# Batch 1's steps, the weight differences, one gate difference and the batch loads at other places in an attention and feed-forward kernel

## The chip, the cores and the metric

One core of a Trainium2 chip runs the kernel. The metric is the time of one execution on the device, in microseconds (us); the median of three runs stands for a kernel. Beside it there is a profiled execution, whose trace gives the start and the length of every instruction. The engines are PE (matrix products), ACT (activation functions and copies), DVE (elementwise work and reductions), POOL (elementwise work, and the issue of DMAs that convert types) and SP (the issue of the other DMAs). Each engine works through its own instructions in the order of the program, and waits for others by semaphores.

## The reference

```python
def _attn_ref(q, k, v):                      # 8 batches, 8 heads, 576 tokens, 64 per head
    q_s = np.exp(q - np.max(q, axis=-1, keepdims=True))
    q_s = q_s / (np.sum(q_s, axis=-1, keepdims=True) + 1e-09)
    k_s = np.exp(k - np.max(k, axis=2, keepdims=True))
    k_s = k_s / (np.sum(k_s, axis=2, keepdims=True) + 1e-09)
    kv = np.einsum('bhsd,bhse->bhde', k_s, v)
    return np.einsum('bhsd,bhde->bhse', q_s, kv)

def _moe_ref(x, w_in, w_out, beta):          # x: (4608, 512), the heads side by side
    h = x @ w_in                             # w_in: (512, 2048)
    g = h * (1.0 / (1.0 + np.exp(-beta * h)))
    return g @ w_out                         # w_out: (2048, 512)
```

## The kernel before

The 576 tokens of a batch are 512 main tokens and a remainder of 64. The feed-forward part runs over nine slabs of 512 tokens: slab t (0 to 7) holds the main tokens of batch t, slab 8 the remainders of all eight. The attention of batch t + 1 is worked out while slab t runs, so that its result XT (the input of the slab, four pieces of 128 columns) is there when slab t + 1 starts.

**A slab.** Pass 1 (line 618) makes 16 tiles of the hidden layer, each by four matmuls of 512 columns; ACT applies the activation (GT), DVE multiplies by 1/beta (`scale_g`, L633) and adds up tiles into GS1 and GS2 (`g_sum1`, `g_sum2`). Pass 2 of slab 0 is a plain output product of 64 matmuls (`pass2_group`). In the other slabs pass 2 (`pass2_fast`, line 695) is a Strassen-like scheme of seven products of 16 matmuls (256 columns, L703). It uses sums of quarters of WOUT (WSUM, made by `w_sum`, L685), differences of quarters (`w_diff`, L691, in place in WOUT) and differences of halves of GT (`g_diff`, L673, in place in GT). The first three products use GS1 and GS2, the fourth and fifth untouched quarters of GT. The sixth needs `g_diff(0)`, the seventh `g_diff(1)`. DVE collects three products in TS (L754, L757, L761).

**The attention of a batch.** The main tokens of q, k and v are loaded to QF, KF and VF (`load_main`), the remainders to QRF, KRF and VRF. ACT takes exponentials (EQ, EK, EKR, EQR). `norm_main` normalises the queries of two head pairs: a reduce (L331) and a reciprocal (L332) on DVE, a multiply (L333) on POOL or DVE. The normalised queries are transposed to QT by PE for batches 1 and 2 (`t_steps`, with a copy on ACT), by a DMA from SP for later ones (`turn`, L482); the query remainders go to QTR (`turn_rem`, L489). `cast_v` casts v to VB, `cast_vr` its remainder. `kv_steps` are the key-value products; behind each pair DVE takes a reciprocal (RC, L437) and scales (KVD, L417). `out_step` multiplies KVD by QT, and DVE or ACT evacuates the result to XT (L455). `outr_steps` does the same for the remainders of two batches, with QTR, into XT8.

**What sets the order.** The whole program is one list, written in the order of emission; each engine gets its part of it. Attention steps have due places in ticks, in the list `todo`: a matmul of pass 1 and one of slab 0's output product count one tick, one of `pass2_fast` 32/56 (so a product is 9.14 ticks, and pass 2 is ticks 64 to 128). After each matmul `tick` emits the steps that are due. `spread(steps, lo, hi)` gives steps even places from lo to hi. `on(n, f)` hangs other work at place n of pass 2: `at(0)` is its start, `at(1)` stands behind the second product and the copy of the first, `at(3)` behind the third product, `at(4)` to `at(7)` behind the following ones. Loads are issued in program order by SP, which waits at each until the buffer is free. The lines that the change touches are the due places (506 to 519 and 795 to 811), the gate differences in `pass2_fast` (763), the weight differences and casts of v (820 to 837), the end of slab 0 (844 to 862), and the hooks (884 to 918).

## Time and profile before

| | |
|---|---|
| median of 3 runs | 293.38 us (293.07 to 293.47) |
| the profiled execution | 295.68 us |
| its span in the trace | 293.9 us |
| TensorE clock granted, mean of the span | 0.983 |
| HBM read / written | 36.71 MB / 9.44 MB |
| slowest DMA of a batch load, issue to landing (VF, 1 MB) | 10.9 us (median of 6) |

The span runs from the first to the last instruction of the trace; the time of the execution holds what lies around it too. Rows of the timeline read: start and length in us, engine, line, operation, out<-in, shape, count, and in brackets how long the engine was idle ahead of it and which instruction ended that. PEld is the loading of weights into PE, which runs beside PE. Rows of the list of waits read: total us, how many times, the longest. SPq and POOLq are the issuing of DMAs. A buffer's number is left out of its name.

### The profile page before, as it was taken

The page shows a single profiled execution, that of the slowest core. Times are in us where ns is not written, and L with a number is a line of the kernel's source. Part 1 is how long each engine was busy: PE and PEld are TensorE (multiplying, and loading weights), DVE is VectorE, ACT ScalarE, POOL GpSimd, SP SyncE. Part 2 cuts the span into 40 slices and gives each one's busy share as a digit, 9 for nine tenths or more (in the row PEclk, how much of TensorE's full clock was granted, in tenths as well). Part 3 has the DMA queues.
Part 4 walks back from the last instruction along what each step waited for, and adds up shares of the span by engine and source line. Part 5 has one row for each costly group of instructions (what it writes and reads, how often), then busy time and mean ns, then how long its engine had stood idle before and what let it go on. Part 6 is the DMA issues. An engine that isn't in the chain of part 4 may idle for free.

```text
span 293.9 us, 4673 instructions
## 1 busy us (share of the span) xinstructions
PE 272.2 (93%) x1819; PEld 168.9 (57%) x1845; DVE 198.9 (68%) x408; ACT 186.1 (63%) x284; POOL 70.6 (24%) x84
## 2 busy tenths in 40 slices
PE   7899968998799979999894999999999999999994
PEld 2444424457654766458551587568656854784583
DVE  5953594499746896987844678697768747654851
ACT  4787574898468954789562695688567457218610
POOL 2870070353600094600830007200600100000000
PEclk9999999999999998999997899999999999999999
DMA  7999999997960069955999004701430040003005
GB/s 219 307 206 206 269 340 349 227 354 256 333 194 0 0 92 347 244 180 186 273 349 249 0 8 94 171 0 39 88 144 2 0 163 0 2 0 143 2 1 142
DMA packets 57205, 45.39 MB, mean 154 GB/s; under 512 B 26448, under 2 KB 56160, under 8 KB 56160
## 3 DMA queue, kind: packets, MB, share of 16 engines
q1 hardware_dynamic: 52352, 40.38, 48.3%
q0 software_dynamic: 4224, 4.19, 8.6%
q10 hardware_dynamic: 608, 0.53, 0.5%
q8 instruction: 14, 0.23, 0.3%
q14 instruction: 7, 0.06, 0.1%
HBM read 36.71 MB, written 9.44 MB: 157 GB/s over the span
## 4 chain that ended last, share of the span: by engine, by line
PE 62%; DVE 16%; DMA 10%; POOL 3%; ACT 3%; SPq 3%; issue 2%; POOLq 0%
PE PS L375 36%; PE PS L703 25%; DMA QF<-in_q_dram 5%; DMA WOUT<-in_moe_w_out_dram 4%; DVE QS L331 4%; DVE GT L673 4%; SPq L482 2%; DVE KVD L417 1%; DVE GT L633 1%; ACT GT L627 1%; POOL VB L348 1%; DMA QTR<-EQR 1%; DVE GS L666 1%; POOL WIN L548 1%; ACT EQ L300 1%
## 5 line engine op out<-in xcount | busy, mean ns | idle before, releaser
L375 PE MATMUL PS<-XT,WIN 128*128 128x512 bf16 x559 | 130.8, 384 | 1.8 <-DVE XT L455 0.8
L627 ACT ACTIVATE GT<-PS,BETA 128x512 bf16<-128x512 f32 x144 | 98.9, 688 | 46.8 <-PE PS L375 46.8
L375 PEld LDWEIGHTS PS<-XT,WIN 128*128 128x128 bf16 x576 | 53.5, 98 | 62.6 <-DVE XT L455 2.3
L633 DVE TENSOR_SCALAR GT<-GT,RB 128x512 bf16<-128x512 bf16 x144 | 54.2, 390 | 45.3 <-ACT GT L627 44.8
L333 POOL TENSOR_TENSOR EQ<-EQ,QI 128x1024 bf16<-128x1024 bf16 (+1 forms) x17 | 28.9, 1702 | 123.9 <-DVE QI L332 106.7
L703 PE MATMUL PS<-WOUT,GT 128*128 128x256 bf16 x256 | 35.1, 273 | 4.5 <-DVE RC L437 3.7
L703 PE MATMUL PS<-WSUM,GT 128*128 128x256 bf16 x256 | 32.2, 280 | 0.0
L703 PE MATMUL PS<-WOUT,GS 128*128 128x256 bf16 x256 | 30.3, 273 | 0.2
L703 PEld LDWEIGHTS PS<-WSUM,GT 128*128 128x128 bf16 x256 | 25.7, 101 | 4.7 <-issue 0.3
L703 PEld LDWEIGHTS PS<-WOUT,GS 128*128 128x128 bf16 x256 | 24.9, 98 | 3.6
L703 PEld LDWEIGHTS PS<-WOUT,GT 128*128 128x128 bf16 x256 | 24.8, 98 | 3.6 <-DVE TS L757 0.2
L733 ACT COPY O2S<-PS 128x512 f32<-128x512 f32 x16 | 9.3, 584 | 25.0 <-PE PS L703 23.5
L331 DVE TENSOR_REDUCE QS<-EQ 128x16 f32<-128x1024 bf16 (+1 forms) x20 | 19.9, 994 | 4.4 <-ACT EQ L300 4.4
L673 DVE TENSOR_TENSOR GT<-GT 128x2048 bf16<-128x2048 bf16 x16 | 22.6, 1453 | 0.0
L375 PE MATMUL PS<-VB,EK 128*128 128x129 bf16 x128 | 21.3, 220 | 1.2 <-DVE VB L348 1.1
L666 DVE TENSOR_TENSOR GS<-GT 128x512 bf16<-128x512 bf16 (+2 forms) x32 | 22.3, 697 | 0.0
L300 ACT ACTIVATE EQ<-QF 128x512 bf16<-128x512 f32 x32 | 17.9, 619 | 6.3 <-DMA QF<-in_q_dram 6.3
L455 ACT CAST XT<-PS 128x512 bf16<-128x512 f32 x18 | 10.4, 582 | 16.8 <-PE PS L375 16.7
L741 DVE TENSOR_TENSOR O2S<-TS,PS 128x512 f32<-128x512 f32 x16 | 10.7, 679 | 13.4 <-PE PS L703 13.4
L348 POOL CAST VB<-VF 128x512 bf16<-128x512 f32 x24 | 18.1, 752 | 1.9
L300 ACT ACTIVATE EK<-KF 128x512 bf16<-128x512 f32 x32 | 18.0, 617 | 0.3 <-DMA KF<-in_k_dram 0.3
L703 PE MATMUL PS<-WSUM,GS 128*128 128x256 bf16 x128 | 16.6, 274 | 1.0 <-DVE GS L661 0.8
(77 smaller groups left out, 240.5 us busy)
## 6 DMA issues: line engine op xcount, KB each, us to landing
out_dram<-O2S SPq DMA_DIRECT2D x8, 1024.0 KB, 4.1
QF<-in_q_dram SPq DMA_DIRECT2D x6, 1024.0 KB, 7.0
KF<-in_k_dram SPq DMA_DIRECT2D x6, 1024.0 KB, 8.6
VF<-in_v_dram SPq DMA_DIRECT2D x6, 1024.0 KB, 10.9
KF<-in_k_dram SPq DMA_DIRECT2D x8, 256.0 KB, 5.6
VF<-in_v_dram SPq DMA_DIRECT2D x8, 256.0 KB, 5.6
WIN<-in_moe_w_in_dram POOLq DMA_DIRECT2D x4, 512.0 KB, 7.4
WOUT<-in_moe_w_out_dram POOLq DMA_DIRECT2D x4, 512.0 KB, 15.6
```

Source lines behind the costliest of these rows:

```text
L300: add(ACTE, lambda e, o=o, a=a: e.activation(o, a, ACT.Exp), r=[(name + "f", i, hp)], w=[("e" + name, i, hp)])
L331: add(DVE, lambda e: e.tensor_reduce(s_, a, AX.X, ALU.add), r=ks, w=[("qs", i, hp0)])
L333: add(eng, lambda e: e.tensor_tensor(a, a, vb, ALU.mult), r=ks + [("qi", i, hp0)], w=ks)
L348: add(eng, lambda e: (e.copy if eng == ACTE else e.tensor_copy)(o, a), r=[("vf", i, hp), ("vone", i)], w=[("vb", i, hp)])
L375: add(PE, lambda e: e.matmul(o, l, r_, start=start, stop=stop), r=r, w=w, bank=[bk])
L455: add(eng, lambda e: (e.copy if eng == ACTE else e.tensor_copy)(XT[i][:, hp, :], PS[bk][:, :]), r=[("ps", bk)], w=[("xt", i, hp)], bank=[bk])
L627: add(ACTE, lambda e: e.activation(GT[:, f, :], PS[bk][:, :], ACT.Silu, scale=BETA[:, f:f + 1]), r=[("ps", bk), "beta"], w=[("gt", f, 0), ...
L633: add(DVE, lambda e: e.tensor_scalar(GT[:, f, :], GT[:, f, :], RB[:, f:f + 1], None, ALU.mult), r=k + ["rb"], w=k)
L666: add(DVE, lambda e: e.tensor_tensor(GS2[:, i:i + n, :], GT[:, i:i + n, :], GT[:, i + NG:i + NG + n, :], ALU.add), r=[k_ for f in (i, i + ...
L673: add(DVE, lambda e: e.tensor_tensor(gv(f, th, NG), gv(f, th, NG), gv(f, 1 - th, NG), ALU.subtract), r=gk(f, 0, NG) + gk(f, 1, NG), w=gk(f ...
L703: add(PE, lambda e, l=l, r_=r_, st=st, u=u, i=i: e.matmul(PS[bk][:, 256 * u:256 * u + 256], l, r_, start=st, stop=end and i == NG - 1, ski ...
L741: add(DVE, lambda e: e.tensor_tensor(o, ts, bank3(bk), ALU.add), r=["ts", ("ps", bk)], w=w, bank=[bk])
```

## The change

In slab 0, batch 1's steps go from ticks 89 to 127 to ticks 104 to 126 of the output product, with the last two key-value and output steps behind it; its query load waits for the third piece of WOUT, not the first; two weight sums go ahead of its norms. In slab 1 both weight differences go ahead of pass 1. In slabs 1 and 2 `norm_main` goes one hook later, `g_diff(0)` stands behind the norms and `g_diff(1)` behind the key-value scalings, by a due place of its own; batch 2's steps and the last steps of batches 3 and 4 move by some ticks. Batch 3's casts of v wait until slab 2 has scaled its first tile. In slab 3 the exponentials of batch 5's keys, its casts, the load of batch 6 and the query remainders go later, behind batch 5's norms and transposes; the load of batch 7 goes to slab 4. The remainder products of batches 2 and 3 (`outr_steps(3)`) go from ticks 40 to 56 to ticks 72 to 88 of slab 4.

```diff
-        def cast_v(b, hp, eng=POOL):
+        def cast_v(b, hp, eng=POOL, after=()):
...
-                r=[("vf", i, hp), ("vone", i)], w=[("vb", i, hp)])
+                r=[("vf", i, hp), ("vone", i)], w=[("vb", i, hp)], after=after)
...
             if b == 2:
-                s = spread(t_steps(b, (0, 1), MB, ACTE), 96, 99) + spread(k01, 99, 102)
-                s += spread(k23, 102, 106) + spread(t_steps(b, (2, 3), MB, ACTE), 108, 111)
-                return s + spread(x[0:2], 107, 108) + spread(x[2:4], 116, 120)
+                s = spread(t_steps(b, (0, 1), MB, ACTE), 104, 107) + spread(k01, 107, 110)
+                s += spread(k23, 110, 113) + [(113.5, lambda: g_diff(1))] + spread(x[0:2], 114, 116)
+                s += spread(t_steps(b, (2, 3), MB, ACTE), 116.5, 119)
+                return s + spread(x[2:4], 122, 125)
             if b == 3:
-                return (spread(k01, 97, 101) + spread(k23, 101, 105) + spread(x[0:2], 109, 112)
-                        + spread(x[2:4], 119, 122))
-            return spread(k01, 92, 98) + spread(k23, 98, 104) + spread(x, 108, 122)
+                s = spread(k01, 97, 101) + spread(k23, 101, 105) + [(105, lambda: g_diff(1))]
+                return s + spread(x[0:2], 110, 113) + spread(x[2:4], 120, 123)
+            return spread(k01, 93, 97) + spread(k23, 97, 101) + spread(x, 105, 122)
...
-            g_diff(0)
-            g_diff(1)
+            if t not in (1, 2):
+                g_diff(0)
+                g_diff(1)
...
-                        for hp, x in enumerate((89, 95, 100, 105))]
-                todo += [(101, one(exp_kr_s, 1))]
...
+                        for hp, x in enumerate((105, 110, 114, 117))]
+                todo += [(104, one(exp_kr_s, 1))]
...
-                    todo += spread(outr_steps(2 * t - 5), 40, 56) if t < 6 else spread(
-                        outr_steps(7), 60, 76)
+                    todo += spread(outr_steps(2 * t - 5), *((72, 88), (40, 56), (60, 76))[t - 4])
...
-            elif t == 2:
-                for hp in range(NHP):
-                    cast_v(3, hp)
+                w_diff(0)
+                w_diff(1)
...
-                    if t == 1 and n in (5, 10):
-                        w_diff(n // 10)
+                    if t == 2 and n == 2:
+                        for hp in range(NHP):
+                            cast_v(3, hp, after=P.writer[("gt", 0, 0)])
...
-                load_main("qf", qt_h, QF, 1, split=4, after=P.writer[("wout", 3, 0)])
+                load_main("qf", qt_h, QF, 1, split=4, after=P.writer[("wout", 11, 0)])
...
+                w_sum(0)
+                w_sum(2)
                 for hp in range(NHP):
                     norm_main(1, hp, 1, POOL if hp else DVE)
-                w_sum(0)
-                w_sum(2)
...
             if t == 1:
...
-                on(1, norm_main, 2, 0, 2, POOL)
-                on(2, norm_main, 2, 2, 2, POOL)
+                on(2, norm_main, 2, 0, 2, POOL)
+                on(3, norm_main, 2, 2, 2, POOL)
+                on(3, g_diff, 0)
             elif t == 2:
                 on(0, exps, 3)
-                on(1, norm_turn, 3, 0)
-                on(2, norm_turn, 3, 2)
+                on(2, norm_turn, 3, 0)
+                on(3, norm_turn, 3, 2)
+                on(3, g_diff, 0)
...
+            elif t == 3:
+                on(0, exp_k, 4)
+                on(0, exp_kr, 4)
+                on(0, exp_q, 5)
+                on(3, norm_turn, 5, 0)
+                on(4, norm_turn, 5, 2)
+                on(5, exp_k, 5)
+                on(5, exp_qr)
+                on(5, casts, 5)
+                on(5, load, 6)
+                on(7, norm_turn_rem)
+                on(7, load_rem, "qrf", qt_h, QRF, 4)
...
-                if b + 2 < B:
-                    on(0, load, b + 2)
+                if t == 4:
+                    on(0, load, 7)
```

Three places show how the instructions move. The first is DVE's order in slab 0, from the last scaled tiles to the first cast of v (before).

```order
L633 TENSOR_SCALAR GT<-GT,RB 128x512 x2
L331 TENSOR_REDUCE QS<-EQ 128x8
L332 RECIPROCAL QI<-QS 128x8
L333 TENSOR_TENSOR EQ<-EQ,QI 128x512
L331 TENSOR_REDUCE QS<-EQ 128x8
L332 RECIPROCAL QI<-QS 128x8
L331 TENSOR_REDUCE QS<-EQ 128x8
L332 RECIPROCAL QI<-QS 128x8
L331 TENSOR_REDUCE QS<-EQ 128x8
L332 RECIPROCAL QI<-QS 128x8
L685 TENSOR_TENSOR WSUM<-WOUT 128x2048 x2
```

The same place of DVE in the changed kernel:

```order
L634 TENSOR_SCALAR GT<-GT,RB 128x512 x2
L686 TENSOR_TENSOR WSUM<-WOUT 128x2048 x2
L331 TENSOR_REDUCE QS<-EQ 128x8
L332 RECIPROCAL QI<-QS 128x8
L333 TENSOR_TENSOR EQ<-EQ,QI 128x512
L331 TENSOR_REDUCE QS<-EQ 128x8
```

The two weight sums, which read all of WOUT, moved from behind the norms of batch 1's queries to ahead of them.

The second is DVE's order in pass 2 of slab 2, from the copy of the first product (before).

```order
L754 COPY TS<-PS 128x512
L331 TENSOR_REDUCE QS<-EQ 128x16
L332 RECIPROCAL QI<-QS 128x16
L757 TENSOR_TENSOR TS<-TS,PS 128x512
L331 TENSOR_REDUCE QS<-EQ 128x16
L332 RECIPROCAL QI<-QS 128x16
L761 TENSOR_TENSOR TS<-TS,PS 128x512
L673 TENSOR_TENSOR GT<-GT 128x8x256 x2
L437 RECIPROCAL RC<-PS 128x2
L417 SCALAR_TENSOR_TENSOR KVD<-PS,RC,MASK 128x128 x2
```

In the changed kernel DVE has there:

```order
L755 COPY TS<-PS 128x512
L758 TENSOR_TENSOR TS<-TS,PS 128x512
L331 TENSOR_REDUCE QS<-EQ 128x16
L332 RECIPROCAL QI<-QS 128x16
L762 TENSOR_TENSOR TS<-TS,PS 128x512
L331 TENSOR_REDUCE QS<-EQ 128x16
L332 RECIPROCAL QI<-QS 128x16
L674 TENSOR_TENSOR GT<-GT 128x8x256
L437 RECIPROCAL RC<-PS 128x2
L417 SCALAR_TENSOR_TENSOR KVD<-PS,RC,MASK 128x128 x2
```

One gate difference stands ahead of the key-value scalings, where there were two; the other follows the second pair of scalings. Each norm's reduce and reciprocal moved behind one more subtraction.

The third is SP's order from the store of slab 2's output (`out_dram`) to that of slab 3's (before).

```order
L643 DMA out_dram<-O2S 128x2048
L268 DMA QF<-in_q_dram 128x8x256
L268 DMA KF<-in_k_dram 128x8x256
L268 DMA VF<-in_v_dram 128x8x256
L275 DMA KRF<-in_k_dram 64x8x64 x2
L275 DMA VRF<-in_v_dram 64x8x64 x2
L275 DMA QRF<-in_q_dram 64x8x64 x2
L268 DMA QF<-in_q_dram 128x8x256
L268 DMA KF<-in_k_dram 128x8x256
L268 DMA VF<-in_v_dram 128x8x256
L482 DMA_TRANSPOSE QT<-EQ 128x8x128 x2
L489 DMA_TRANSPOSE QTR<-EQR 128x4x128
```

In the changed kernel SP has there:

```order
L644 DMA out_dram<-O2S 128x2048
L482 DMA_TRANSPOSE QT<-EQ 128x8x128 x2
L268 DMA QF<-in_q_dram 128x8x256
L268 DMA KF<-in_k_dram 128x8x256
L268 DMA VF<-in_v_dram 128x8x256
L275 DMA KRF<-in_k_dram 64x8x64 x2
L275 DMA VRF<-in_v_dram 64x8x64 x2
L489 DMA_TRANSPOSE QTR<-EQR 128x4x128
L275 DMA QRF<-in_q_dram 64x8x64 x2
L644 DMA out_dram<-O2S 128x2048
```

The transposes of batch 5's queries moved ahead of the load of batch 6; the remainder's transpose stays behind it; the load of batch 7 follows the store.

More of the change, by code (lines that the diff above doesn't have):

```diff
@@ L795, in bass_efficient_attn_shen__then__act_swish_beta_kernel @@
                 todo = [(x, steps(t_steps, 1, (hp,), NOW, ACTE))
-                        for hp, x in enumerate((89, 95, 100, 105))]
-                todo += [(101, one(exp_kr_s, 1))]
-                todo += [(x, one(exp_k, 1, hp, 1)) for hp, x in enumerate((102, 106, 111, 116))]
-                todo += [(x, one(cast_v, 1, hp, DVE)) for hp, x in enumerate((104, 107, 112, 118))]
+                        for hp, x in enumerate((105, 110, 114, 117))]
+                todo += [(104, one(exp_kr_s, 1))]
+                todo += [(x, one(exp_k, 1, hp, 1)) for hp, x in enumerate((111, 115, 118, 122))]
+                todo += [(x, one(cast_v, 1, hp, DVE)) for hp, x in enumerate((112, 117.5, 120, 125))]
                 todo += [(x, steps(kv_steps, 1, (hp,), NOW))
-                         for hp, x in enumerate((109, 115, 121, 127))]
-                todo += [(x, steps(out_step, 1, hp, NOW, ACTE)) for hp, x in enumerate((119, 125))]
+                         for hp, x in enumerate((116, 119, 124))]
+                todo += [(x, steps(out_step, 1, hp, NOW, ACTE)) for hp, x in enumerate((121, 126))]
             elif t < 4:
@@ L858, in bass_efficient_attn_shen__then__act_swish_beta_kernel @@
                     todo.pop()[1]()
+                go(kv_steps(1, (3,), NOW))
                 go(out_step(1, 2, NOW, ACTE))
```

10 lines of the change are left out of this document (1 added, 9 removed).

## The prediction

> **What bounds the kernel now.** I read the page first, then the list of waits of PE, then the timeline at every place where PE stood still.
>
> ```profile
> PE 272.2 (93%) x1819; PEld 168.9 (57%) x1845; DVE 198.9 (68%) x408; ACT 186.1 (63%) x284; POOL 70.6 (24%) x84
> PE PS L703 <- DVE RC L437: 3.7, 2, 2.2
> PE PS L375 <- DMA QTR<-EQR: 3.7, 1, 3.7
> PE PS L373 <- POOL EQ L333: 1.6, 2, 1.1
> PE PS L375 <- DVE VB L348: 1.1, 2, 0.7
> ```
>
> PE works for 93% of the span, so PE bounds the kernel, and what can be gained is its waits and the time it runs at a lower clock. The next rows are the first product of pass 2 in slabs 1 to 4, and, from the chain of work, in slab 5.
>
> ```profile
> 65.11 2.00 PE L703 MATMUL PS<-WSUM,GS 128*128 128x256 bf16 x14
> 97.32 2.05 PE L703 MATMUL PS<-WSUM,GS 128*128 128x256 bf16 x16
> 129.73 2.05 PE L703 MATMUL PS<-WSUM,GS 128*128 128x256 bf16 x16
> 167.04 2.05 PE L703 MATMUL PS<-WSUM,GS 128*128 128x256 bf16 x16
> 195.61 4.07 PE PS L703 x36
> ```
>
> From one to the next it is 32.2, 32.4, 37.3 and 28.6 us. The last one has no wait worth a line, so about 28.6 us is what a slab needs, and the first three lose 3.6, 3.8 and 8.7. The clock is part of it (columns: stretch, length, busy time and count of PE, PEld, DVE, ACT, POOL, granted clock, DMA share, GB/s):
>
> ```profile
> 111.00:112.00 1.00, 1.00 (x7) 0.69 (x6) 0.00 (x0) 0.54 (x1) 0.94 (x2) 0.50 1.04 359
> 163.00:164.00 1.00, 1.00 (x5) 0.36 (x3) 0.39 (x2) 0.54 (x1) 0.00 (x0) 0.50 0.00 0
> ```
>
> Behind the two longest waits (2.2 and 3.7 us) PE runs at half clock; stretch by stretch it is from 109.7 to 113.1 and from 159.0 to 164.3, so 1.7 and 2.6 us are lost on top of the waits.
>
> **Slab 0.** Batch 1's steps now stand behind 41 matmuls of the output product. What comes with it: batch 1's queries load behind the third piece of WOUT, not the first, and DVE adds the two weight sums, which need the last piece, ahead of the four query norms.
>
> ```profile
> L554 POOL DMA_DIRECT2D WOUT<-in_moe_w_out_dram x4: 770/781/795, 14.4 to 16.6; - x4
> DMA to landing us min/median/max: 12.5/15.6/20.3
> 30.16 5.56 PE L375 MATMUL PS<-WOUT,GT 128*128 128x512 bf16 x24
> 29.62 1.22 DVE L685 TENSOR_TENSOR WSUM<-WOUT 128x2048 bf16<-128x2048 bf16 x1
> 39.41 3.54 DVE L685 TENSOR_TENSOR WSUM<-WOUT 128x2048 bf16<-128x2048 bf16 x2
> 33.95 0.69 DVE L331 TENSOR_REDUCE QS<-EQ 128x8 f32<-128x512 bf16 x1 [2.52 <-ACT EQ L300]
> 35.66 0.23 PEld L373 LDWEIGHTS PS<-IDB,EQ 128*128 128x128 bf16 x4 [0.44 <-DVE EQ L333]
> ```
>
> PE's waits in front of batch 1's transposes (1.6 on POOL, 0.44 on DVE) and of its first key-value product (0.7) go, 2.7 us in all. The pieces of WOUT land from 26.9 (14.4 + 12.5) to 36.9 (16.6 + 20.3), 3.3 apart, with 1 MB of queries moving among them. Without those I take 2.7 apart (if the shares went by bytes, 1.5 MB of WOUT to 1 MB of queries, it would be 2.0): third at 32.3, last at 35.6 once the queries run beside it. DVE then ends the sums at 35.6 + 2 x 1.22 = 38.1 and the first norm (1.7 from its reduce at 33.95 to the transpose that waited for it, at 35.66) at 39.8. PE, at 0.217 a matmul, reaches the transpose at 30.2 + 41 x 0.217 = 39.1: it waits 0.7. The second norm ends on POOL 0.6 after PE wants it, and the remainder cast VRS, behind three multiplies on POOL, is 0.7 late. So 2.0 is added for 2.7 removed. With the last piece at 36.9 as now it is 3.3, and with the sums at 3.54 us 4.4. **Term: 0**, between a gain of 2.7 and a loss of 3.4 (the last with a half-clock stretch).
>
> **Slab 1.** The weight differences leave the busy end of pass 1 for its start.
>
> ```profile
> 56.88 1.21 DVE L691 TENSOR_TENSOR WOUT<-WOUT 128x2048 bf16<-128x2048 bf16 x1
> 53.08 0.35 DVE L633 TENSOR_SCALAR GT<-GT,RB 128x512 bf16<-128x512 bf16 x1 [1.85 <-ACT GT L627]
> 67.91 0.39 PE L703 MATMUL PS<-WSUM,GS 128*128 128x256 bf16 x2 [0.80 <-DVE GS L661]
> 77.92 0.27 PE L703 MATMUL PS<-WOUT,GT 128*128 128x256 bf16 x1 [1.49 <-DVE RC L437]
> L673 DVE TENSOR_TENSOR GT<-GT x4: 1624/2157/2691, 72.9 to 107.2; 128x2048 bf16<-128x2048 bf16 x4
> 135.92 2.35 DVE L673 TENSOR_TENSOR GT<-GT 128x2048 bf16<-128x2048 bf16 x2
> ```
>
> Two of 1.21 us go into a gap of 1.85; the 0.6 over is made up in the 0.5 us that DVE is idle at each following tile, so the wait of 0.80 goes. In pass 2 both gate differences stand ahead of the key-value scalings that PE waits for: 4.3 us together while POOL multiplies and casts, 2.35 where POOL is idle (135.92). After the change one stands ahead, and PE's wait of 1.49 goes with 0.4 of shorter ones behind it. The second difference, now uncontended since batch 3's casts moved to slab 2, ends about when its product wants it, and delays the next evacuation, for which PE waits some 0.5. **Term: -2.2**, between -1.2 and -2.6.
>
> **Slab 2.** Same move, with transposes by DMA.
>
> ```profile
> 104.28 3.48 SPq L482 DMA_TRANSPOSE QT<-EQ  x2
> QT<-EQ SPq DMA_TRANSPOSE x1, 4.5
> 102.35 3.88 POOL L333 TENSOR_TENSOR EQ<-EQ,QI 128x1024 bf16<-128x1024 bf16 x2 [23.43 <-DVE QI L332]
> 133.57 0.69 DVE L757 TENSOR_TENSOR TS<-TS,PS 128x512 f32<-128x512 f32 x1 [1.05 <-PE PS L703]
> 102.67 1.21 DVE L331 TENSOR_REDUCE QS<-EQ 128x16 f32<-128x1024 bf16 x1
> 116.33 3.57 PEld L375 LDWEIGHTS PS<-XT,WIN 128*128 128x128 bf16 x18 [0.63 <-DVE XT L455]
> ```
>
> Now the norm stands behind the first subtraction, which starts 3.84 after the pass (133.57 - 129.73), at 101.2. DVE in a row: subtraction 0.7, reduce 1.2, reciprocal 0.25, and the same again, to 105.4; one gate difference 2.1, to 107.5; the scalings 1.5, to 109.0; the second difference 1.2 to 2.1; then evacuation 0.6, 0.7, reduce 1.2, reciprocal 0.25, evacuation 0.6: the last input tile of slab 3 is there at 113.6 to 114.5, now 116.3. PE meanwhile wants the transposed queries at 107.3: their multiply ends 1 us later than now, at 105.2, and the transpose takes 3.3 to 4.5 us, so PE waits till 108.6 to 109.8, then has 4.3 us of work, which ends at 112.9 to 114.1, so DVE's chain is later. **Term: -1.8**; -2.7 if the second difference is fast, -0.3 if the clock halves again.
>
> The Trainium skill, page "SBUF — State Buffer", section "Who interferes with whom", says that a VectorE instruction with two SBUF inputs and a GpSimd one that reads SBUF exclude each other for a whole instruction, and this speaks against the change, since the remaining difference starts together with POOL's multiply. By that rule the difference would end 1.0 us later whenever POOL's 1.94 us came first, and the sum would be 1 us worse; the four differences of the row above took 1.6 to 2.7 us, and I stay with their middle.
>
> **Slabs 3 and 4.** In slab 3 batch 4's output step comes three ticks (0.6 us) earlier, but what it waits for does not.
>
> ```profile
> 140.46 0.38 PE L703 MATMUL PS<-WOUT,GT 128*128 128x256 bf16 x2 [0.78 <-DVE KVD L417]
> 147.73 8.70 SPq L482 DMA_TRANSPOSE QT<-EQ  x2
> QT<-EQ SPq DMA_TRANSPOSE x1, 9.7
> 156.47 1.27 SPq L489 DMA_TRANSPOSE QTR<-EQR  x1
> 159.01 0.23 PE L375 MATMUL PS<-QTR,KVD 128*128 128x64 bf16 x1 [3.67 <-DMA QTR<-EQR]
> 145.41 1.89 PE L375 MATMUL PS<-XT,WIN 128*128 128x512 bf16 x8
> 180.48 7.88 PE PS L375 x49
> 77.37 2.90 SPq L275 DMA_DIRECT2D VRF<-in_v_dram  x2
> 69.52 0.37 SPq L268 DMA_DIRECT2D QF<-in_q_dram  x1
> ```
>
> PE's wait there grows as much as the later wait of 0.44 shrinks, and the four key exponentials and the remainder's (2.8 us on ACT) now stand ahead of the last evacuation: **+0.4**, at most +1.5. Slab 4 is the large one. Pass 1 takes 167.04 - 145.41 = 21.6 us there and 195.61 - 180.48 = 15.1 in slab 5, with the same work: the 6.5 between them are the wait of 3.67 for the transposed remainder and the half clock behind it. The remainder's products now stand at tick 72, in pass 2, and the transposes of batch 5 no longer queue behind two batch loads on SP. PE will be at tick 72 at 145.8 + 15.0 + 1.5 = 162.3. On SP the remainder's transpose now follows one whole load, issued from about 145.2; the same loads in slab 1 took from 69.5 to 80.3 to issue, so it goes out at 156.0 and lands 2.5 us later, as at 156.47, or up to 9.7 later, as the transpose issued at 147.73 behind three loads. I take 160.5, in time. Batch 6's casts on POOL now fall beside the end of pass 1, for which I allow 0.3. **Term: -6.2**, or next to nothing if it lands at the slow end.
>
> **Sum.** 0 - 2.2 - 1.8 + 0.4 - 6.2 = -9.8: the span goes from 293.9 to 284.1. The profiled execution took 295.68 us, the median of the runs shown is 293.38; the difference of 2.3 I leave as it is, so the forecast is 293.4 - 9.8 = **283.6 us**. Slabs 5 to 8 stay as they are.
>
> **Rivals.** (1) *The weight sums hold up batch 1.* With WOUT's last piece at 36.9 and the sums at 3.54, PE waits 36.9 + 3.5 + 1.7 - 39.1 = 3.0 at the first transpose and 1.4 behind it, and a half-clock stretch costs 1.7: slab 0 loses 3.4, 287.0 us. For it: the sums wait for the last piece by construction; against it: the queries no longer share the DMA with the third piece. (2) *Slab 2 keeps its half clock*, since the transposes replace the scalings as the wait: 1.5 worse, 285.1. For it speaks that the 4.5 us landing alone makes 2.4 us of wait; against it that the wait of 1.49 in slab 1 left the clock at 1.00. (3) *The remainder's transpose lands at the slow end*, 165.7: a wait of 3.4 and 2.6 of half clock give 6.0 back, 289.6. (4) *Slower than before by that same wait*: all is lost when the remainder lands 7.2 us (9.8 less 2.6) past tick 72, at 169.5, which needs the transpose stuck on SP till 160 behind loads whose ring is full; at 171 the time is 294.9. (5) *The waits only change names* and each engine's total stands: 293.4.
>
> The Trainium skill, page "TensorE: Matmul & The Clock Gate", section "Part 1: The HAM clock gate (the "warmup" mystery)", has the half clock come after at least one idle window of about 3.4 us. Here 2.2 us of waiting were enough (clock 0.50 at 111), so by that rule the stretch in slab 2 had another cause and would stay: 1.5 us more, the same as rival 2.
>
> **How the numbers follow.** Forecast 0.60 (281.5 to 285.5: the terms of slabs 0, 1 and 2, each uncertain by about 1 and independent, make 2 either way), rival 1 0.13, rival 2 0.10, rival 3 0.12, rival 4 0.03, rival 5 0.02. The range of 280.5 to 288.5 holds the forecast and rivals 1 and 2; downward it goes half the way to the best bounds of slabs 0, 1, 2 and 4 together (-2.7 - 2.6 - 2.7 - 6.5 = -14.5, without the 0.4, 278.9). About 0.2% is what a measurement of this kernel can tell from no change. Faster is everything but rivals 4 and 5: 0.95; same 0.02; slower 0.03.
>
> **What would show it.** Right: in the waits of PE no line for QTR, the lines for RC gone or under 0.5 us, clock 1.00 everywhere from slab 1 on, and 30.0, 30.6 and 31.5 us between the first products of slabs 1 to 4. Wrong: PE waiting for norms in slab 0 by more than 2.5 us, a clock of 0.50 in any slab, or QTR still named.

## The result, and the profile after

The changed kernel took **284.73 us** (median of 4, 284.34 to 285.11), the kernel before, run beside it, 293.43 (293.07 to 294.58): a ratio of 0.9697, 95% interval 0.9667 to 0.9727. The profiled execution took 284.34 us with a span of 282.5, so the two profiled executions differ by 11.34 us and the two medians by 8.7. That gap is taken up in the experiments.

First comes PE's row on the page of the changed kernel, and then rows of its list of waits (total us, times, longest):

```profile
PE 270.2 (96%) x1845; PEld 168.6 (60%) x1845; DVE 195.1 (69%) x408; ACT 186.1 (66%) x284; POOL 67.6 (24%) x84
```

```profile
PE PS L375 <- DVE KVD L417: 2.3, 4, 1.2
...
PE PS L375 <- DMA QT<-EQ: 1.2, 2, 0.9
PE PS L704 <- DVE GS L662: 1.1, 2, 0.7
PE PS L375 <- DVE VB L348: 0.9, 2, 0.5
```

No row of the list names QTR, RC or POOL's EQ any more. From pass 2 of slab 1 on, what is left is 0.7 us for the sums of GT in slab 1, 0.9 and 0.3 for the transposed queries in slab 2, and 1.2 for the scalings in slab 3, beside two waits of 0.2 and 0.35. The timeline of PE has the first products of pass 2 in slabs 1 to 5:

```profile
63.71 1.69 PE L704 MATMUL PS<-WSUM,GS 128*128 128x256 bf16 x14
...
94.39 2.05 PE L704 MATMUL PS<-WSUM,GS 128*128 128x256 bf16 x16
...
124.11 2.05 PE L704 MATMUL PS<-WSUM,GS 128*128 128x256 bf16 x16
...
155.06 1.69 PE L704 MATMUL PS<-WSUM,GS 128*128 128x256 bf16 x14
...
184.09 2.05 PE L704 MATMUL PS<-WSUM,GS 128*128 128x256 bf16 x16
```

In the kernel before, the first product of slab 5 is this one; the row of 195.61 that the prediction took for it, from the chain of work, starts 0.16 us behind it:

```profile
195.45 2.05 PE L703 MATMUL PS<-WSUM,GS 128*128 128x256 bf16 x16
```

From these and the rows of before comes this table (us; the first line is from the start of the span to the first product of slab 1, the others go from one first product to the next):

| | before | after | difference | predicted |
|---|---|---|---|---|
| slab 0 and pass 1 of slab 1 | 65.1 | 63.7 | -1.4 | 0 |
| slab 1 | 32.2 | 30.7 | -1.5 | -2.2 |
| slab 2 | 32.4 | 29.7 | -2.7 | -1.8 |
| slab 3, with pass 1 of slab 4 | 37.3 | 31.0 | -6.4 | -5.8 with the next line |
| pass 2 of slab 4, with pass 1 of slab 5 | 28.4 | 29.0 | +0.6 | |
| the rest | 98.4 | 98.4 | 0.0 | 0 |

Two rows by stretch follow (columns as in the prediction; the granted clock is the third number from the end). They lie in slabs 2 and 4, where before had its half clock:

```profile
109.00:113.00 4.00, 4.00 (x26) 2.35 (x24) 3.77 (x8) 3.25 (x4) 3.38 (x4) 1.00 1.02 351
156.00:160.00 4.00, 3.65 (x38) 2.95 (x37) 2.61 (x6) 3.99 (x7) 2.90 (x5) 1.00 0.99 322
```

It is 1.00 in both, and in the mean of the whole span.

### The profile page after: what moved, and what is told of

Same layout as the page of the kernel before. It is cut to its first block, busy times and chain, and to the rows that moved or that the text cites. A ratio compares the mean times of both kernels' runs of the same rounds, so it can differ in the third digit from the quotient of the medians.

```text
span 282.5 us, 4705 instructions
## 1 busy us (share of the span) xinstructions
PE 270.2 (96%) x1845; PEld 168.6 (60%) x1845; DVE 195.1 (69%) x408; ACT 186.1 (66%) x284; POOL 67.6 (24%) x84
## 4 chain that ended last, share of the span: by engine, by line
PE 71%; DVE 10%; DMA 9%; POOL 4%; ACT 1%; SPq 1%; issue 1%; POOLq 0%
PE PS L375 41%; PE PS L704 30%; DMA WOUT<-in_moe_w_out_dram 5%; POOL EQ L333 2%; DVE GT L634 2%; DMA VF<-in_v_dram 2%; DVE GS L667 2%; DVE GS L662 2%; DVE QS L331 1%; DMA QT<-EQ 1%; POOL WIN L549 1%; SPq L268 1%; DVE GT L674 1%; ACT GT L628 1%; ACT QT L393 1%
## 5 line engine op out<-in xcount | busy, mean ns | idle before, releaser
L333 POOL TENSOR_TENSOR EQ<-EQ,QI 128x1024 bf16<-128x1024 bf16 (+1 forms) x17 | 29.8, 1753 | 94.6 <-DVE QI L332 74.2
L704 PE MATMUL PS<-WOUT,GT 128*128 128x256 bf16 x256 | 33.6, 273 | 0.0
L704 PEld LDWEIGHTS PS<-WSUM,GT 128*128 128x128 bf16 x256 | 24.9, 98 | 4.1 <-issue 0.2
L375 PE MATMUL PS<-VB,EK 128*128 128x129 bf16 x128 | 20.7, 220 | 1.1 <-DVE VB L348 0.9
L674 DVE TENSOR_TENSOR GT<-GT 128x2048 bf16<-128x2048 bf16 x16 | 19.3, 1239 | 0.0
L348 POOL CAST VB<-VF 128x512 bf16<-128x512 f32 x24 | 16.4, 684 | 9.6 <-DVE GT L634 7.8
```

Of the source, the lines that this page charges most:

```text
L333: add(eng, lambda e: e.tensor_tensor(a, a, vb, ALU.mult), r=ks + [("qi", i, hp0)], w=ks)
L348: add(eng, lambda e: (e.copy if eng == ACTE else e.tensor_copy)(o, a), r=[("vf", i, hp), ("vone", i)], w=[("vb", i, hp)], after=after)
L375: add(PE, lambda e: e.matmul(o, l, r_, start=start, stop=stop), r=r, w=w, bank=[bk])
L674: add(DVE, lambda e: e.tensor_tensor(gv(f, th, NG), gv(f, th, NG), gv(f, 1 - th, NG), ALU.subtract), r=gk(f, 0, NG) + gk(f, 1, NG), w=gk(f ...
L704: add(PE, lambda e, l=l, r_=r_, st=st, u=u, i=i: e.matmul(PS[bk][:, 256 * u:256 * u + 256], l, r_, start=st, stop=end and i == NG - 1, ski ...
```

## The experiments

All times are medians; the kernel before ran beside each. In the changed kernel slab 1 takes 30.68 us, slab 2 29.72, slab 3 30.95 and slab 4 29.03, from first product to first product; the slabs of the experiments are measured in the same way.

**1. The kernel before again.** No edit.

> The kernel before, unchanged, to see the granted clock of each of its executions. The profiled execution of before took 295.7 us at a mean clock of 0.983 with two half-clock stretches (slabs 2 and 4), while its median is 293.4. Theory A: the stretches come in some executions and not in others, so times and clocks go together: about 293 us at 0.99 or more, 295 to 296 us at 0.983. Theory B: both stretches come every time: the clock is 0.983 in all executions, and what spreads the times by 2 us is something else.

Measured: 294.57 us (293.2 to 296.5; ratio 1.0013, 0.9981 to 1.0046). These 12 executions and the 54 of before that ran beside this and the later experiments fall into four groups:

| granted clock | executions | us |
|---|---|---|
| 0.998 | 2 | 291.7 to 291.8 |
| 0.992 to 0.994 | 12 | 293.1 to 293.6 |
| 0.986 to 0.988 | 29 | 293.9 to 295.4 |
| 0.983 | 23 | 295.6 to 296.5 |

With the 1.7 and 2.6 us that the prediction read off for the two half-clock stretches, the groups are: neither stretch (291.7), the short one of slab 2 (291.7 + 1.7 = 293.4), the long one of slab 4 (294.3), both (296.0). The profiled execution of this run has 0.988. PE's wait in slab 2, and then two stretches, show which of the two it has:

```profile
109.68 0.38 PE L375 MATMUL PS<-QT,KVD 128*128 128x512 bf16 x1 [1.98 <-DVE KVD L417]
```

```profile
109.00:112.00 3.00, 2.32 (x20) 1.91 (x21) 2.04 (x8) 1.07 (x2) 2.68 (x5) 1.00 0.81 198
...
158.00:161.00 3.00, 3.00 (x11) 1.20 (x12) 0.29 (x1) 0.69 (x1) 0.00 (x0) 0.50 0.74 306
```

Slab 2 (109 to 112) runs at full clock behind a wait of 1.98 us, slab 4 at half. Theory A holds. Other profiles fit the groups: 0.983 with both stretches in the kernel before and in run 4, 0.992 with the short one alone in run 2. By the groups the short stretch came in 35 of 66 executions and the long one in 52. The prediction's profile had both; the median of 293.38 that it started from lies where an execution with the short stretch alone lies, and so it was a low draw too: the median of the 66 is 294.5.

The same row shows that one of the prediction's signs says little. The kernel is unchanged, and yet this wait names KVD where the profile of before named RC. That profile has 26 matmul records fewer (1819 of 1845), and this first matmul of QT and KVD is one that it lacks, so the wait is put down there to what released the next one, 0.21 us later: its 2.19 us are the 1.98 of here, and its 1.49 in slab 1 is 1.28.

The Trainium skill, page "TensorE: Matmul & The Clock Gate", section "Part 1: The HAM clock gate (the "warmup" mystery)", says that the window over which activity is judged runs freely, so that one kernel meets it at different places from run to run. These 66 executions fit that, with four groups for one kernel, though no run here shows the window itself. That a whole idle window of about 3.4 us is needed, they do not bear out: 1.98 us were enough in the profiled execution of the next run.

**2. Slabs 3 and 4 alone, and 3. one edit of them alone.** The kernel before with the hooks, loads and due places of slabs 3 and 4 as changed, in short

```diff
+            elif t == 3:
...
+                on(3, norm_turn, 5, 0)
+                on(4, norm_turn, 5, 2)
...
+                on(5, load, 6)
+                on(7, norm_turn_rem)
...
+                if t == 4:
+                    on(0, load, 7)
```

together with the edit that follows, and the kernel before with this edit only:

```diff
-                    todo += spread(outr_steps(2 * t - 5), 40, 56) if t < 6 else spread(
-                        outr_steps(7), 60, 76)
+                    todo += spread(outr_steps(2 * t - 5), *((72, 88), (40, 56), (60, 76))[t - 4])
```

> The kernel before with the changed slabs 3 and 4 alone (the hooks of slab 3, the load of batch 7 in slab 4, the remainder products at ticks 72 to 88, the last due places). If the part is worth what the two profiled executions differ by (slabs 3 and 4 together 6.4 us), the time is 293.4 - 6.4 = 287.0 us. If a good part of the half-clock stretch behind the long wait is missing in the usual execution of the kernel before, only the wait of 3.7 goes and the time is 289 to 290 us. No wait for QTR in either case.

> The kernel before with one edit, the remainder products of batches 2 and 3 at ticks 72 to 88 of slab 4, and the loads and transposes in their old order. In the profile of before the transposed remainder lands at about 159.0, 13.6 us behind the start of pass 1 of slab 4, and tick 72 comes some 16.5 us behind it. Theory C (the later place of the products alone takes the wait away): the same time as with all of slabs 3 and 4 changed, within 0.5 us, and no wait for QTR. Theory D (it needs the transposes ahead of the loads on SP): a wait for QTR of over 1 us stays and the time is over 1 us above that kernel's.

Measured: 288.70 us (ratio 0.9809, 0.9776 to 0.9842) and 289.13 (0.9811, 0.9777 to 0.9845). The first lies between the two values that were set for it, 287.0 and 289 to 290, and the pair shows theory C. Neither profile has a wait for QTR. The whole gain of slabs 3 and 4 comes from the later place of the remainder products. The other edits there cost something: the first pair of rows is PE's first products of slabs 3 to 5 with all of them, the second with the one edit.

```profile
129.72 2.05 PE L703 MATMUL PS<-WSUM,GS 128*128 128x256 bf16 x16
...
160.68 1.69 PE L703 MATMUL PS<-WSUM,GS 128*128 128x256 bf16 x14
...
189.84 2.05 PE L703 MATMUL PS<-WSUM,GS 128*128 128x256 bf16 x16
```

```profile
128.15 2.05 PE L703 MATMUL PS<-WSUM,GS 128*128 128x256 bf16 x16
...
158.78 1.94 PE L703 MATMUL PS<-WSUM,GS 128*128 128x256 bf16 x15
...
187.42 2.05 PE L703 MATMUL PS<-WSUM,GS 128*128 128x256 bf16 x16
```

Slab 3 is 30.96 us against 30.63, and slab 4 is 29.16 against 28.64: 0.85 us are lost. The medians hide it, because four of six executions with the one edit had a clock of 0.993 to 0.994 (289.1 to 289.5 us; the two at 1.000 took 287.7), and one of five with all edits was as low as 0.992 (290.1; the others 288.4 to 288.7). At like clocks the kernel with all edits is 0.6 to 1.0 us slower, as the traces have it.

**4. Slab 0 alone.** The kernel before with batch 1's steps at the changed ticks, and

```diff
-                load_main("qf", qt_h, QF, 1, split=4, after=P.writer[("wout", 3, 0)])
+                load_main("qf", qt_h, QF, 1, split=4, after=P.writer[("wout", 11, 0)])
...
+                w_sum(0)
+                w_sum(2)
                 for hp in range(NHP):
                     norm_main(1, hp, 1, POOL if hp else DVE)
-                w_sum(0)
-                w_sum(2)
...
+                go(kv_steps(1, (3,), NOW))
```

> The kernel before with the changed slab 0 alone (batch 1's steps at ticks 104 to 126, its queries loaded behind the third piece of WOUT, two weight sums ahead of the norms). The prediction's term for it is 0, so 293.4 us; the profiled executions differ by 1.4 us up to the first product of slab 1, so 292.0 us. Rival: the weight sums hold up the transposes of batch 1 when they stand alone, and the time is above 294.

Measured: 293.50 us, ratio 0.9962 (0.9936 to 0.9989): a gain of about 1.1 us by the ratio, and 0.5 to 0.9 when executions of the same granted clock on the same chip are compared. In the profile, pass 1 of slab 1 starts at 50.26, in run 1 at 51.33, so 1.07 earlier. But slab 1 takes 32.81 us against 32.37, since PE now waits 1.54 us there for the sums (GS), where it waited 1.09: a part of the gain is lost again at once. The rows behind that are those of PE in run 1 and here:

```profile
68.10 0.39 PE L703 MATMUL PS<-WSUM,GS 128*128 128x256 bf16 x2 [0.80 <-DVE GS L661]
```

```profile
66.30 0.39 PE L703 MATMUL PS<-WSUM,GS 128*128 128x256 bf16 x2 [0.74 <-DVE GS L661]
...
67.49 0.39 PE L703 MATMUL PS<-WSUM,GS 128*128 128x256 bf16 x2 [0.80 <-DVE GS L661]
```

In run 1 the wait of 0.74 is one of 0.29. For slab 0 itself, the term was not 0.

**5. The weight differences back.** The changed kernel with

```diff
-                w_diff(0)
-                w_diff(1)
...
+                    if t == 1 and n in (5, 10):
+                        w_diff(n // 10)
```

> The changed kernel (284.7 us) with the two weight differences of slab 1 back behind tiles 5 and 10 of pass 1. In the changed kernel the first product of slab 1 still waits 0.71 us for the sums of GT, at a place where DVE has had no idle time for the last 8 us. Theory A (the differences do cost there what DVE has no room for: most of the second one's 1.2 us, less what it shields from POOL's casts): the product waits 0.4 to 1.2 us longer, 285.1 to 285.9 us. Theory B (the wait comes from POOL's casts alone): no change, 284.5 to 284.9.

Measured: 285.67 us (285.43 to 285.87; ratio 0.9702, 0.9666 to 0.9738), 0.94 above the changed kernel, in slab 1 alone (31.67 against 30.68). The waits for GS are 0.73 and 0.80 us, where the changed kernel has one of 0.71. Theory A: moving them was worth about 1 us, and yet a wait stayed.

**6. Batch 2's casts behind the sums.** The changed kernel with

```diff
-                for hp in range(NHP):
-                    cast_v(2, hp)
...
+                if t == 1 and n == NF:
+                    for hp in range(NHP):
+                        cast_v(2, hp, after=P.writer[("gs1", NG - 1)])
```

> The changed kernel with batch 2's four casts of v on POOL held back until the last sum of GT in slab 1. Beside them four scalings of DVE took 0.58 us each, where 0.35 is usual, 0.9 us in all. Theory A (this contention is what is left of the wait for GS): the wait of 0.71 falls under 0.2 and the time by about 0.5, to 284.2 us. Rival: the casts now stand ahead of the norms' multiplies on POOL, PE waits for POOL EQ or VB in slab 1 instead, and the time is 284.7 or more.

Measured: 284.13 us (284.0 to 284.72; ratio 0.9651, 0.9618 to 0.9684), 0.6 under the changed kernel; slab 1 takes 29.93. In the changed kernel the timelines of POOL and DVE near the end of pass 1 of slab 1 read:

```profile
58.76 3.79 POOL L348 CAST VB<-VF 128x512 bf16<-128x512 f32 x4
```

```profile
60.64 2.31 DVE L634 TENSOR_SCALAR GT<-GT,RB 128x512 bf16<-128x512 bf16 x4
```

and with the casts held back:

```profile
60.38 0.87 DVE L634 TENSOR_SCALAR GT<-GT,RB 128x512 bf16<-128x512 bf16 x3
61.52 0.35 DVE L634 TENSOR_SCALAR GT<-GT,RB 128x512 bf16<-128x512 bf16 x1 [0.26 <-ACT GT L628]
```

A scaling takes 0.58 us beside POOL's casts and 0.29 to 0.35 without them, and the wait for GS in slab 1 is gone. Theory A.

**7. The norms of slab 2 one hook earlier.** The changed kernel with

```diff
-                on(2, norm_turn, 3, 0)
-                on(3, norm_turn, 3, 2)
+                on(1, norm_turn, 3, 0)
+                on(2, norm_turn, 3, 2)
```

> The changed kernel with the norms and transposes of slab 2 one hook earlier, as in the kernel before; the gate difference stays behind the key-value scalings. Theory A (the wait for the transposed queries, 0.92 and 0.27 us, is there because the norm stands behind a subtraction): POOL's first multiply starts 1.1 to 1.3 us earlier, both waits go, the fourth product waits up to 0.2 for the subtraction, and the time falls by 0.8 to 1.0, to 283.8 us. Rival: the last pieces of XT, not the transposes, set the end of slab 2, and the time stays within 0.3 of 284.7.

Measured: 285.20 us (284.81 to 285.66; ratio 0.9685, 0.9652 to 0.9719). The theory fell: both waits for QT went, but slab 2 takes 29.87 us against 29.72. The reason stands in two engines' timelines. POOL and DVE here:

```profile
99.76 3.88 POOL L333 TENSOR_TENSOR EQ<-EQ,QI 128x1024 bf16<-128x1024 bf16 x2 [13.65 <-DVE QI L332]
```

```profile
102.03 2.69 DVE L674 TENSOR_TENSOR GT<-GT 128x2048 bf16<-128x2048 bf16 x1
104.65 0.16 DVE L437 RECIPROCAL RC<-PS 128x2 f32<-128x2 f32 x1
```

In the changed kernel DVE has

```profile
102.20 1.26 DVE L674 TENSOR_TENSOR GT<-GT 128x2048 bf16<-128x2048 bf16 x1
```

and its chain of waits, through POOL and the DMA to PE:

```profile
100.47 1.91 POOL EQ L333
...
102.45 2.77 POOL EQ L333
...
105.24 3.14 DMA QT<-EQ
```

Whichever of the two starts first is done in its own time, and the other waits for it. In the changed kernel the gate difference starts at 102.20, ahead of POOL's second multiply (102.45), takes 1.26, and the multiply takes 2.77 where 1.91 is usual. It starts first because it stands right behind the reciprocal that the multiply waits for; here, and in the kernel before, a subtraction of 0.63 us stands between the two. With the norms earlier the multiply is running when the difference comes, the difference takes 2.69, and PE waits 1.30 us for the scalings behind it. The Trainium skill, page "SBUF — State Buffer", section "Who interferes with whom", says just this: the two exclude each other for a whole instruction, and the order of issue decides who is blocked. Here the trace agrees, with 2.69 and 1.26 for the same instruction.

The medians differ by 0.5 us, the two profiled executions by 1.3. Of that, 0.4 is lost ahead of the first product of slab 1, and 0.8 in slab 4, which this edit does not touch: the first product waits there 1.15 us for GS, in the changed kernel 0.35. Pass 2 starts 0.5 us later (155.55), but batch 6's casts on POOL start when their load has landed (154.31, in the changed kernel 154.38), and so meet more of the last scalings. That this is the cause was not tested alone; in run 12, where these casts stand behind the sums, slab 4 has no wait for GS.

**8. The second gate difference of slab 3 behind the scalings.** The changed kernel with

```diff
-            if t not in (1, 2):
-                g_diff(0)
-                g_diff(1)
+            if t not in (1, 2):
+                g_diff(0)
+            if t not in (1, 2, 3):
+                g_diff(1)
...
+            return (spread(k01, 93, 97) + spread(k23, 97, 101) + [(101, lambda: g_diff(1))]
+                    + spread(x, 105, 122))
```

> The changed kernel with the second gate difference of slab 3 moved behind the key-value scalings too, as slabs 1 and 2 have it. In the changed kernel PE waits 1.21 us there for KVD, with 2.35 us of gate differences ahead of it on DVE. Theory A (the difference is the cause): the wait falls to about 0.1 and the time by 1.1, to 283.6 us. Rival: the second difference now ends too late for the seventh product or the last evacuation, and at least half is given back: 284.2 or more.

Measured: 286.77 us (286.25 to 288.66; ratio 0.9754, 0.9713 to 0.9795), 2.0 slower than the changed kernel: the rival. The wait for KVD falls to 0.30, but the difference now starts inside POOL's multiply. Rows of POOL, DVE and PE:

```profile
135.53 1.90 POOL L333 TENSOR_TENSOR EQ<-EQ,QI 128x1024 bf16<-128x1024 bf16 x1 [0.18 <-DVE RC L437]
```

```profile
135.97 2.54 DVE L675 TENSOR_TENSOR GT<-GT 128x2048 bf16<-128x2048 bf16 x1
138.44 1.28 DVE L455 CAST XT<-PS 128x512 bf16<-128x512 f32 x2
```

```profile
139.18 0.39 PE L375 MATMUL PS<-QT,KVD 128*128 128x512 bf16 x1 [1.72 <-DVE XT L455]
```

The evacuations behind it are late, PE waits 1.72, and slab 3 takes 31.72 against 30.95. Slab 4 loses another 1.4, with waits for GS of 0.75 and 0.80 beside the casts of batch 6. Two of the six executions had a clock of 0.993 and took 288.6 us.

**9. Both gate differences ahead again in slabs 1 and 2.** The changed kernel with

```diff
-                s += spread(k23, 110, 113) + [(113.5, lambda: g_diff(1))] + spread(x[0:2], 114, 116)
+                s += spread(k23, 110, 113) + spread(x[0:2], 114, 116)
...
-                s = spread(k01, 97, 101) + spread(k23, 101, 105) + [(105, lambda: g_diff(1))]
+                s = spread(k01, 97, 101) + spread(k23, 101, 105)
...
                 on(3, g_diff, 0)
+                on(3, g_diff, 1)
```

(the last for both slabs).

> The changed kernel with both gate differences back ahead of the key-value scalings in slabs 1 and 2, everything else as changed. The prediction has the wait of 1.5 us in slab 1 and of 2.2 us in slab 2 gone because the second difference stands behind the scalings. Theory A (that is the mechanism): PE waits for KVD again, 1.2 to 2.7 us in each of the two slabs, by whether POOL's multiply runs beside the second difference, and the time goes to 287.0 to 289.5 us, a half-clock stretch in slab 2 included. Rival (the later norms made the room, and the place of the difference matters little): under 286 us.

Measured: 286.92 us (286.22 to 288.38; ratio 0.9757, 0.9704 to 0.981), 2.2 slower than the changed kernel. PE's timeline has

```profile
77.09 0.38 PE L375 MATMUL PS<-QT,KVD 128*128 128x512 bf16 x1 [0.87 <-DVE KVD L417]
...
108.09 0.38 PE L375 MATMUL PS<-QT,KVD 128*128 128x512 bf16 x1 [2.24 <-DVE KVD L417]
```

The mechanism is theory A's in both slabs (31.49 against 30.68, and 30.88 against 29.72), though the wait of slab 1 and the time are a little under its numbers. Another 0.9 us is lost in slab 4, where the first product waits 1.27 us for GS. One of the six executions had a clock of 0.994 and took 288.4.

**10. Three edits at once.** Run 6's edit; batch 6's casts (main and remainder) behind the sums of slab 4 in the same way; and

```diff
-                    todo += spread(outr_steps(2 * t - 5), *((72, 88), (40, 56), (60, 76))[t - 4])
+                    todo += spread(outr_steps(2 * t - 5), *((78, 94), (40, 56), (60, 76))[t - 4])
...
-                on(3, norm_turn, 5, 0)
-                on(4, norm_turn, 5, 2)
+                on(4, norm_turn, 5, 0)
+                on(5, norm_turn, 5, 2)
```

> The changed kernel with three edits: in slab 1 batch 2's casts of v behind the sums of GT (as in the run that did it alone, -0.7 us in slab 1); in slab 4 batch 6's casts behind the sums of GT too; in slab 3 batch 5's norms one hook later, so that two key-value scalings stand ahead of them on DVE, and the remainder products of slab 4 six ticks later. Theory A (PE's waits in slabs 1, 3 and 4 come from DVE's work ahead of the scalings and from POOL's casts beside the sums): the waits of 0.71, 1.21 and 0.35 us fall to 0.3 in all and the time goes to 282.4 to 283.0 us. Rival: POOL's later multiplies and casts meet the gate differences and the last evacuations, or the remainder's transpose lands late, and 1 us or more is given back: 283.8 or more.

Measured: 288.39 us (287.61 to 289.33; ratio 0.9804, 0.9752 to 0.9856), 3.7 slower. Slabs 1 and 3 did what was expected (29.92, and 29.60 against 30.95), but slab 4 takes 35.28. DVE and PE there:

```profile
159.85 2.35 DVE L674 TENSOR_TENSOR GT<-GT 128x2048 bf16<-128x2048 bf16 x2
162.12 1.21 DVE L331 TENSOR_REDUCE QS<-EQ 128x16 f32<-128x1024 bf16 x1
163.37 0.25 DVE L332 RECIPROCAL QI<-QS 128x16 f32<-128x16 f32 x1
163.53 0.63 DVE L474 CAST XT<-PS 128x512 bf16<-128x512 f32 x1
```

```profile
164.31 0.59 PE L375 MATMUL PS<-QT,KVD 128*128 128x512 bf16 x1 [4.09 <-DVE XT L474]
```

Six ticks later the last remainder product comes behind the third product's hook, so its evacuation (L474) stands behind the gate differences and a norm, and PE waits 4.09 us for the bank. From 164 to 168 the clock is 0.50. None of the theories had this. Run 12 undoes these six ticks alone.

**11. Another order in slab 2.** The changed kernel with run 7's edit, and

```diff
-                s = spread(k01, 97, 101) + spread(k23, 101, 105) + [(105, lambda: g_diff(1))]
+                s = spread(k01, 97, 101) + spread(k23, 101, 105) + [(101, lambda: g_diff(0)), (105, lambda: g_diff(1))]
...
-                on(3, g_diff, 0)
...
-                on(4, casts, 4)
...
                 on(7, norm_turn, 4, 2)
+                on(7, casts, 4)
```

> The changed kernel with another order in slab 2: norms and transposes one hook earlier (which alone gave nothing, since the first gate difference then met POOL's second multiply and took 2.69 us, and the scalings behind it were 1.3 us late), the first gate difference behind the first pair of scalings, and batch 4's casts on POOL behind its last norm. Theory A (the collision was what gave it back): no wait for KVD or QT over 0.3 in slab 2, up to 0.5 for the sixth product, and 0.6 us less from the first product of slab 2 to that of slab 3 than the 29.72 us of the changed kernel. Rival: the transposes still land at 105.6 or later, or the sixth product waits over 1 us for the difference: no gain.

Measured: 284.84 us (284.16 to 285.5; ratio 0.968, 0.9625 to 0.9735), no gain: the rival. Both gate differences now take 1.22 and 1.21 us and no wait for KVD is left in slab 2, but the chain of waits has

```profile
101.43 4.72 DMA QT<-EQ
```

and PE waits 1.24 us for it; slab 2 takes 30.11 us. This first transpose goes out 1.0 us earlier than the first one of the changed kernel (102.40 on SP) and lands at 106.15, where that one was there at 105.5. Why it takes 4.7 us here and 3.1 there stays open.

**12. Run 10 with the remainder products at ticks 72 to 88.**

```diff
-                    todo += spread(outr_steps(2 * t - 5), *((78, 94), (40, 56), (60, 76))[t - 4])
+                    todo += spread(outr_steps(2 * t - 5), *((72, 88), (40, 56), (60, 76))[t - 4])
```

> The three edits of the run before (batch 2's and batch 6's casts behind the sums of GT, batch 5's norms one hook later), with the remainder products of slab 4 at ticks 72 to 88 again. In that run slabs 1 and 3 were 0.75 and 1.35 us shorter than in the changed kernel, and slab 4 lost 6 us, since the evacuation of the remainder products stood behind two gate differences and a norm on DVE, and PE waited 4.1 us for its bank. Theory A (the later place of the remainder products is all that gave it back): no wait for XT L474, slab 4 at most as long as in the changed kernel (29.0 us), 282.2 to 282.8 us, faster than both kernels. Rival (the later norms of batch 5 delay the load of batch 6 and with it the transposed remainder past tick 72): a wait for QTR of over 1 us and 283.5 us or more.

Measured: **282.97 us** (282.61 to 283.79; ratio 0.9576, 0.9543 to 0.961), faster than both kernels. PE's list of waits has:

```profile
PE PS L375 <- DMA QT<-EQ: 1.2, 2, 0.9
PE PS L375 <- DMA QTR<-EQR: 0.9, 1, 0.9
PE PS L375 <- POOL VRS L354: 0.9, 1, 0.9
PE PS L375 <- DVE KVD L417: 0.9, 2, 0.4
```

Slabs 1 to 4 take 29.93, 29.70, 29.60 and 29.70 us. The wait for XT L474 is gone, as theory A has it, but the time lies 0.2 above its range and slab 4 is 0.7 longer than in the changed kernel: some of the rival came with it. The transpose of the remainder goes out 0.8 us later than in the changed kernel (151.63, not 150.86), while slab 4's pass 2 starts 1.9 us earlier (153.16, not 155.06), so PE reaches tick 72 0.9 us ahead of it.

## Why the prediction came out as it did

The forecast was 1.1 us under the time, and that is the difference of two larger errors: the terms came to -9.8 where the spans differ by 11.4, 1.6 too little, and the starting point was 2.7 out the other way. That the time came so near the forecast is luck. The gains of slabs 1 to 4 were forecast in the right places, that of slab 0 was not.

- **The starting point** is the step that failed most. "The difference of 2.3 I leave as it is" took 4.3 us of half clock off a median that, by run 1, held only some 1.7 of it. The profiled execution was not a slower copy of those behind the median: it had a stretch that they lacked. The profile before lay 2.3 above its median and the one after 0.4 below its own; 11.3 - 2.7 gives the 8.7 of the medians.
- **Slab 0** (0 predicted, -1.4 by the traces, -1.1 by the profile of run 4) was mis-sized. Its own working removes 2.7 and adds 2.0, which is -0.7; the 0 in its place is a middle between bounds and not a sum. The last piece of WOUT was forecast for 35.6, and DVE starts the sums that need it at 34.24:

```profile
34.24 2.36 DVE L686 TENSOR_TENSOR WSUM<-WOUT 128x2048 bf16<-128x2048 bf16 x2 [2.64 <-DMA WOUT<-in_moe_w_out_dram]
```

  The first norm is then done at 38.2, 1 us ahead of PE, where a wait of 0.7 was forecast. Of the 2.7 us of waits to go, 0.47, 0.20 and 0.2 more for a scaling stand in their place. The 0.7 forecast for the remainder cast (VRS) is only 0.2 in the profile of the changed kernel, but 0.87 to 0.93 in all nine of runs 4 to 12, so that profile is a good draw: its first product of slab 1 comes at 63.71, in the nine at 63.79 to 64.11, and with the old slab 0 at 64.75 to 65.15 (four profiles). The wait of rival 1, 3 us for the first norm, is in none of them. Which of the slab's edits does it was not tried apart.
- **Slab 1** (-2.2 predicted, -1.5) has the step that was wrong in its reason: "so the wait of 0.80 goes". It went to 0.71, as POOL's casts fall beside the scalings that follow (run 6). The move did take 0.8 us of waiting away, but from 1.53 (run 5): with the earlier slab 0 the old order would have waited that much longer (1.54 in run 4), and the prediction worked out the two slabs as if they were independent. The other step, one gate difference past the scalings, was right: the wait of 1.49 is gone and comes back as 0.87 when it is undone (run 9). The 0.5 for the next evacuation did not come.
- **Slab 2** (-1.8 predicted, -2.7) was right in its parts: the transposes did take the place of the scalings as the wait (0.92 and 0.27, where 1.3 to 2.5 was worked out), and the clock stayed at 1.00. The first gate difference was priced at 2.1 us, the middle of four. That middle was never measured: in both slabs of before the first of the pair took 2.69 and the second 1.62. The rows of slab 2 there are:

```profile
104.63 2.69 DVE L673 TENSOR_TENSOR GT<-GT 128x2048 bf16<-128x2048 bf16 x1
107.24 1.62 DVE L673 TENSOR_TENSOR GT<-GT 128x2048 bf16<-128x2048 bf16 x1
```

  Against POOL's multiply the price is set by who starts first (run 7): 2.69 inside the multiply (2.54 in run 8), 1.26 ahead of it. In the changed kernel the difference started first, with 0.25 us to spare.
- **Slabs 3 and 4** (-5.8 predicted, -5.7 by the traces) were right in size. Of the working, +0.4 for slab 3 is 0.33, and slab 4 loses 0.52 where 0.3 was allowed for batch 6's casts, both by runs 2 and 3. That the transposes "no longer queue behind two batch loads" contributes nothing: with the old order of loads there is no wait for QTR either (run 3). Rival 3 appears only in run 12, with 0.9 us.
- Rivals 2, 4 and 5 did not come. Of the marks set, QTR and the clock came out as said; so did RC, which by run 1 would have held for the unchanged kernel as well; of the slabs, 30.0, 30.6 and 31.5 were said, and 30.7, 29.7 and 31.0 came. The lower end of the range does not follow from its working: half the way from 283.6 to 278.9 is 281.2, not 280.5.

## What to carry to other kernels

Before a sum is made against a profiled execution, ask whether that execution is the usual one: a clock stretch that comes only sometimes belongs in the range, not in the term. When work moves on DVE, look at what POOL runs at that moment, since here a few tenths of a microsecond decided which of them waited for the other's instruction. And moving a consumer later is worth it only up to the place where its own evacuation falls behind other work: moving the remainder products to tick 72 gained some 5 us (run 3), and from there to tick 78 cost 5.4 (runs 10 and 12).

## What the runs showed of the hardware

- The same wait brings half clock in one execution and not in another: 1.98 us ahead of the same product in slab 2 was followed by 1.00 in runs 1 and 3 and by half clock in run 2, whose rows of PE and of the stretch read:

```profile
109.47 0.38 PE L375 MATMUL PS<-QT,KVD 128*128 128x512 bf16 x1 [1.98 <-DVE KVD L417]
```

```profile
109.00:112.00 3.00, 2.53 (x12) 1.66 (x13) 1.86 (x6) 1.17 (x2) 2.68 (x5) 0.64 0.85 221
```

- DVE's scalings, with one tensor as input, are held up by POOL as well: 0.58 us each beside casts, 0.29 to 0.35 without them (run 6).
- The first transpose of batch 3's queries landed 3.1 us after its issue in the changed kernel and 4.7 in run 11, where it was issued 1.0 us earlier.
